# Keys on 128 partitions, all seven slots of P turned by DMA, q in 1 KB packets turned by TensorE, and the expert stage spread over later pairs

## The chip, the cores and the metric

One core of one Trainium2 chip runs the whole program. Its compute engines are TensorE (PE in the profile; PEld is its weight load), VectorE (DVE), ScalarE (ACT) and GpSimd (POOL). SyncE (SP) computes nothing here: it issues every DMA, one after the other, and waits on semaphores in that same order. The metric is the device time of one execution in microseconds, the median of several runs. A profiled execution gives the trace.

## The reference, cut to what matters

Attention for 8 batches of 12 heads, 448 positions and head size 64, with an RMS norm on q and k; then, on the heads of a batch joined to 768 columns, an expert block: a product with `w_in` (768 x 1024), a relu, a convolution of three taps along the sequence, a gate, and a product with `w_out` (1024 x 768). All in float32.

```python
q_n, k_n = (rmsnorm(q, g_q), rmsnorm(k, g_k))
scores = scale * np.matmul(q_n, k_n.transpose(0, 1, 3, 2))
scores = scores - np.max(scores, axis=-1, keepdims=True)
attn = np.exp(scores)
attn = attn / (np.sum(attn, axis=-1, keepdims=True) + 1e-09)
attn_out = np.matmul(attn, v)
...
h = np.maximum(x @ w_in, 0.0)
for k in range(K):
    conv_out += conv_w[k][None, None, :] * hp[:, k:k + S, :]
gate = 1.0 / (1.0 + np.exp(-conv_out))
return (h * gate @ w_out).astype(np.float32)
```

## The kernel before, in words

**Pairs.** Two heads are one pair: 48 pairs, 6 to a batch. Both heads of a pair lie beside each other (2 x 64 rows of the array), and the 2 x 448 = 896 query positions of a pair are cut into seven slots of 128. In a float16 product each operand is split into a high and a low half (`hi`, `lo`), and three of the four half products are summed: about 22 bits for three float16 passes.

**One pair.** `load_k` and `load_q` fetch k and q (224 KB each) to 112 partitions, four key positions to a partition (`PB = 112`, `NB = 4`). `square`, `square_sum` and `rsqrt` make the norm's factor, `apply_rms` multiplies with it. Then k goes through PE: `qk_transpose` makes four transposes into one bank, `qk_hi` (ACT or DVE) and `qk_lo` (DVE) take the halves out. For q this holds up to pair 6; from pair 7 on (`nq=7`) q is split first on the input side (`x_cast`, `x_rest`) and turned by a DMA transpose (`x_turn`, 8 blocks of 112 x 128). q is loaded with "(h t p)", so in packets of 256 bytes. `scores` makes the products, `soft_max` the row's maximum (DVE), `soft_exp` the exponentials and their sums (ACT).

**P.** For the product with v the exponentials of a slot (128 queries x 448 keys) have to be turned. Up to pair 9 all seven slots go through PE: `p_transpose` (four float32 transposes), `p_evac` (a copy from the bank to `PT`), and `pv` multiplies in float32, four key blocks of 112. From pair 10 on (`n1=10`) five of the seven slots (`dg=5`) go another way: `p_hi` rounds to float16, `p_lo` takes the rest, both into a buffer `ph` (three of them) padded to 4 + 4 blocks of 128 columns, and `p_turn` turns the buffer by one DMA transpose into `PT`. `pv` then multiplies in float16: three half products x four key blocks x two heads = 24 matmuls of 320 columns. The other two slots still use `p_transpose` and float32 products (8 matmuls of 128 columns).

**The end of a pair.** The sums are inverted, turned by PE (`sum_transpose`), copied to `rT` (`sum_evac`), stored to DRAM (`sum_store`, tile `rd`) and read back spread over 64 rows (`sum_load`, tile `rB`); `x_scale` multiplies the product with them, `x_hi` and `x_lo` split the result for the expert block.

**Expert block.** For each batch, `in_part` (8 chunks of 18 matmuls of 448 columns), the elementwise chain `in_relu` to `in_lo` on DVE, ACT and POOL, then `out_part` (matmuls of 384 columns) and `out_evac`, `out_store`.

**What sets the order.** The program is written step by step by a planner. Each step has a due time (`at(...)`, from `base(n)`, the start of pair n, and numbers in `PH`), the steps that it must follow (`needs`), engines it may run on with a cost (`options`), and latencies (`LAT`). The planner simulates the engines and takes the step that can start first; `BETA` times the due time is added, so that of two ready steps the one due earlier goes first. The result is one fixed order for each engine and for SP; nothing is chosen at run time. `plan_moe` sets the due times of the expert block: it begins `ti` after the end of the batch's last pair, a chunk of `in_part` lasts `si`, a unit of `out_part` lasts `so`, the same in every batch.

## Time and profile before

| | us |
|---|---|
| median of 3 runs | 883.89 (881.51 to 886.46) |
| profiled execution, whole | 889.08 |
| its span on the core | 887.0 |
| start of the first exponential of pair 10 | 188.07 |
| start of the first exponential of pair 47 | 796.58 |

The profile of one execution has three stages. Up to 188 us the weights are loaded and split, and pairs 0 to 9 run with all slots through PE. From 188 to 797 us pairs 10 to 47 run, with the expert block of the earlier batches between them. Behind that stands the expert block of the last batch, nearly alone. Busy time of an engine is the union of its instructions; matmuls are pipelined, so the time of one matmul in the chain of work that ended last is shorter than its own duration. SP's instructions are not counted as busy, but the trace has when it issued each DMA, how long that took, and what it waited for.

### The profile page before, as it was taken

What the parts mean: (1) busy time and instruction counts of PE and PEld (TensorE: products, weight loads), DVE (VectorE), ACT (ScalarE), POOL (GpSimd) and SP (SyncE); (2) the same over time, 40 slices, a digit from 0 to 9 for tenths busy, and PEclk for the clock granted to TensorE, in tenths of its full rate; (3) what the DMA queues carried; (4) which work ended last, traced back from release to release, by engine and by line L of the source; (5) the groups of instructions that cost most, each with busy time, mean ns of one, the idle gap of its engine ahead of it and who ended that gap; (6) DMA issues with size and microseconds to landing.
All of it is one profiled execution on the core that took longest, in us unless ns stands there. A gap on an engine that the chain in (4) does not pass through costs nothing.

```text
span 887.0 us, 18246 instructions
## 1 busy us (share of the span) xinstructions
PE 827.4 (93%) x6260; PEld 478.1 (54%) x6260; DVE 702.6 (79%) x1267; ACT 666.8 (75%) x1543; POOL 591.8 (67%) x721
## 2 busy tenths in 40 slices
...
PEclk9897999999999999999999999999999999999999
DMA  8944442257896798798896998577896896565001
GB/s 256 266 124 140 138 83 66 70 111 150 184 201 133 146 197 182 127 163 149 195 182 129 155 208 161 124 171 152 188 180 128 170 187 143 111 109 113 18 18 54
DMA packets 324072, 128.25 MB, mean 145 GB/s; under 512 B 287012, under 2 KB 322188, under 8 KB 323212
## 3 DMA queue, kind: packets, MB, share of 16 engines
...
## 4 chain that ended last, share of the span: by engine, by line
PE 59%; DVE 10%; POOL 8%; DMA 8%; ACT 7%; issue 5%; SPq 1%; ACTq 0%; POOLq 0%; DVEq 0%
PE bank L895 18%; PE bank L816 16%; PE bank L608 9%; PE bank L651 5%; PE bank L744 5%; PE bank L735 5%; DMA PT<-ph 4%; DMA rB<-rd 2%; PE bank L464 2%; POOL sq L90 2%; DMA qT<-qkf 1%; POOL ph L90 1%; ACT ph L78 1%; POOL wo L296 1%; ACT sq L354 1%
## 5 line engine op out<-in xcount | busy, mean ns | idle before, releaser
L816 PE MATMUL bank<-x,wi 128*128 128x448 f16 x1152 | 241.4, 353 | 0.0
L895 PE MATMUL bank<-wo,gring 128*128 128x384 f16 (+1 forms) x1056 | 204.5, 327 | 0.8 <-DVE kT L482 0.8
L816 PEld LDWEIGHTS <-wi 128*128 128x128 f16 x1152 | 109.8, 98 | 99.7 <-issue 13.0
L895 PEld LDWEIGHTS <-gring 128*128 128x128 f16 (+1 forms) x1056 | 101.2, 99 | 65.5 <-issue 10.4
L608 PE MATMUL bank<-kT,qT 64*128 64x448 f16 x864 | 105.1, 359 | 5.6 <-DVE qT L484 3.9
L90 POOL TENSOR_TENSOR sq<-qkf,st 112x512 f32<-112x512 f32 x88 | 99.5, 1148 | 8.9 <-DVE st L389 7.2
L78 ACT COPY PT<-bank 112x512 f32<-112x512 f32 x138 | 79.8, 584 | 23.4 <-PE bank L651 22.8
L735 PE MATMUL bank<-PT,v 112*64 112x128 f32 (+1 forms) x768 | 78.4, 342 | 1.1 <-ACT PT L78 0.8
L90 POOL TENSOR_TENSOR x<-rB,x 128x448 f16<-128x448 f32 x48 | 51.1, 1064 | 27.4 <-ACT x L78 25.9
L744 PE MATMUL bank<-PT,vp 112*64 112x320 f16 x912 | 68.4, 299 | 0.0
L608 PEld LDWEIGHTS <-qT 64*128 64x128 f16 x864 | 34.5, 95 | 55.8 <-issue 27.5
L367 DVE TENSOR_REDUCE st<-sq 112x16 f32<-112x1024 f32 x48 | 57.7, 1209 | 6.9 <-ACT sq L354 6.7
L493 POOL COPY qz<-qT 64x128 f16<-64x128 f16 x91 | 34.1, 375 | 38.1 <-DMA qT<-qkf 11.3
L735 PEld LDWEIGHTS bank<-PT,v 112*64 112x64 f32 x768 | 43.1, 138 | 28.5 <-issue 17.5
L744 PEld LDWEIGHTS <-vp 112*64 112x64 f16 x912 | 53.0, 110 | 7.3 <-DMA PT<-ph 0.2
L751 DVE TENSOR_TENSOR rB<-bank,rB 128x448 f32<-128x448 f32 x48 | 29.7, 619 | 26.8 <-DMA rB<-rd 13.7
L464 PE MATMUL bank<-ident,sq 112*128 112x112 f32 x220 | 33.2, 276 | 18.2 <-POOL sq L90 17.3
L895 PE MATMUL bank<-wo,wi 128*128 128x384 f16 (+1 forms) x192 | 46.9, 326 | 0.0
L354 ACT ACTIVATE sq<-qkf 112x1024 f32<-112x1024 f32 x36 | 38.1, 1059 | 9.3 <-DMA qkf<-in_q_dram 8.2
L90 POOL TENSOR_TENSOR qkf<-sq,qkf 112x512 f16<-112x512 f32 x30 | 35.2, 1175 | 13.1 <-ACT qkf L78 13.0
L714 DVE SCALAR_TENSOR_TENSOR vp<-v,vsc,vp 112x512 f16<-112x512 f32 x38 | 41.6, 1094 | 0.6 <-ACT vp L82 0.6
L464 PEld LDWEIGHTS bank<-ident,sq 112*128 112x128 f32 x220 | 25.7, 148 | 28.4 <-POOL sq L90 20.2
...
## 6 DMA issues: line engine op xcount, KB each, us to landing
...
PT<-ph SPq DMA_TRANSPOSE x190
rd<-rT SPq DMA_DIRECT2D x48, 3.5 KB
```

Source lines behind the costliest of these rows:

```text
L78: (nc.scalar.copy if e == "ACT" else elementwise(e).tensor_copy)(dst, src)
L90: elementwise(e).tensor_tensor(dst, a, b, op=op)
L354: nc.scalar.activation(sq, old("qkf", n), AF.Square)
L367: nc.vector.tensor_reduce(old("st", m)[:, 0, n - m].rearrange("p i s -> p (i s)"), old("sq", n).rearrange("p i h t d -> p (i h t) d")[..., ...
L464: nc.tensor.transpose(ps[:, t * PB : (t + 1) * PB], x[:, t], ident[:PB, :PB])
L608: nc.tensor.matmul(ps[u][:, :S], lhs, kt[r, w], start=(i == 0), stop=(i == 2))
L651: nc.tensor.transpose(ps[:PB, kt * P : (kt + 1) * P], e[:, kt * PB : (kt + 1) * PB], ident)
L714: nc.vector.scalar_tensor_tensor(vp[:, 1], old("v", n), old("vsc", n // NP)[:PB, 1:2], vp[:, 0], op0=ALU.mult, op1=ALU.subtract,)
L735: nc.tensor.matmul(ps[HALF[h], out[h]], v[:, h, k], pt[:, k, col[h]], start=(k == 0), stop=(k == NB - 1),)
L744: nc.tensor.matmul(ps[HALF[h], out[h]], v[:, w, h, k], pt[:PB, a, k, col[h]], start=(i == 0 and k == 0), stop=(i == 2 and k == NB - 1),)
L816: nc.tensor.matmul(ps[:, :S], wi[:, wl, c, fc * P : (fc + 1) * P], old("x", b * NP + c)[:, xl], start=(i == 0), stop=(i == 3 * NP - 1),)
L895: nc.tensor.matmul(ps[p0 : p0 + m, :NO2], g, wo[:, wl, fc, half * NO2 : (half + 1) * NO2], start=(i == 0), stop=(i == 3 * NFC - 1),)
```

## The change

Five things are changed, and with them numbers of the planner.

1. **Keys on 128 partitions.** k and v of a head are no longer four positions on 112 partitions each. The first 256 positions lie on partitions 0 to 63 (four each), the other 192 on partitions 64 to 127 (three each). A load of k becomes two DMAs; a load of v becomes three, since the fourth place of the upper partitions is filled with a copy. A key block is now 128 keys (three and a half blocks), so `qk_transpose` of k makes three transposes of 128 and one of 64, `p_transpose` works on 128 keys at a time, and float32 `pv` takes only the upper half of the last block. Buffers of k and q are fixed (`qkbuf`), and the places that no load fills are zeroed once at the start.
2. **All seven slots by DMA** from pair 10 on (`dg=7`): no `p_transpose`, no `p_evac` and no float32 product there. The buffer holds 3.5 + 3.5 blocks, so `p_turn` moves 7 blocks of 128 and not 8; `p_lo` becomes two instructions of 384 and 64 columns. `pv` becomes 11 matmuls a head, 22 a pair, of 448 columns. There are four `ph` buffers, not three.
3. **q through PE in all pairs** (`nq=100`): `x_cast`, `x_rest` and `x_turn` are gone, `qk_transpose`, `qk_hi` and `qk_lo` of q take their place. q is then loaded with "(h p t)", in packets of 1 KB.
4. **The expert stage spread**: `si` and `so` are multiplied by numbers of each batch (`si0` to `si7`, `so0` to `so7`, up to 1.79), and `so` grows from 6.862 to 8.54.
5. **Small**: three `rB` buffers, not two; `g_rows`, `cw_in` and `cw_rows` lie in the end of `gring`; costs in `options`, some `LAT` entries and `PH` numbers.

```diff
-    ... nf=2, ... dg=5, n1=10, ... nq=7, nk=97, ... so=6.862
+    ... nf=3, ... dg=7, n1=10, ... nq=100, nk=97, ... so=8.54
+    si0=1.0, si1=1.6, si2=1.625, si3=1.415, si4=1.633, si5=1.364, si6=1.149, si7=1.079,
+    so0=1.0, so1=1.536, so2=1.613, so3=1.631, so4=1.791, so5=1.264, so6=1.071, so7=1.0,
...
-        rB=2, ... ph=3, vp=2,
+        rB=3, ... ph=4, vp=2,
...
-    phbuf = [const.tile([P, 2, 4, P], F16, name=f"ph{i}") for i in range(BUFS["ph"])]
+    phbuf = [const.tile([P, 2 * S], F16, name=f"ph{i}") for i in range(BUFS["ph"])]
+    qkbuf = [const.tile([P, 2, 2, 4, D], F32, name=f"qk{i}") for i in range(BUFS["qkf"])]
...
     def load_k(n):
-        queue("lk").dma_start(x[:, 1], kf[rows].rearrange("(h p t) d -> p h t d", h=2, t=NB))
+        for i, m in enumerate((4, 3)):
+            queue("lk").dma_start(
+                x[HALF[i], 1, :, :m],
+                src[:, 256 * i : 256 * i + 64 * m].rearrange("h (p t) d -> p h t d", t=m),
+            )
...
     def load_q(n):
-            old("qkf", n)[:, 0], qf[rows].rearrange("(h t p) d -> p h t d", h=2, t=NB)
+        order = "(h t p) d -> p h t d" if turned(n, 0) else "(h p t) d -> p h t d"
+            old("qkf", n)[:PB, 0], qf[rows].rearrange(order, h=2, t=NB),
...
     def v_load(n):
-        queue("lv").dma_start(t, vf[rows].rearrange("(h p t) d -> p h t d", h=2, t=NB))
+        for i, m in enumerate((4, 3)):
+            queue("lv").dma_start(
+                t[HALF[i], :, :m],
+                src[:, 256 * i : 256 * i + 64 * m].rearrange("h (p t) d -> p h t d", t=m),
+            )
+        queue("lv").dma_start(
+            t[HALF[1], :, 3], src[:, :256].rearrange("h (p t) d -> p h t d", t=4)[:, :, 3]
+        )
...
     def p_lo(n, j):
-        binary(
-            on["p_lo", n, j], ph[:, 1, :, :PB],
-            old("e", (n, j)).rearrange("q (k p) -> q k p", k=NB), ph[:, 0, :, :PB], ALU.subtract,
-        )
+        for k0, k1, to in ((0, 3 * P, 4 * P), (3 * P, S, S)):
+            binary(
+                on["p_lo", n, j], ph[:, to : to + k1 - k0], e[:, k0:k1], ph[:, k0:k1],
+                ALU.subtract,
+            )
...
-    PV3 = ((0, 0), (0, 1), (1, 0))
+    PV7 = (
+        ((0, 0, P), (1, 0, P), (2, 0, P), (3, 0, P)),
+        ((0, 1, P), (1, 1, P), (2, 1, P), (3, 1, 64)),
+        ((4, 0, P), (5, 0, P), (6, 0, P)),
+    )
...
     def plan_moe(b):
-        si, so = PH["si"], PH["so"]
+        si, so = PH["si"] * PH[f"si{b}"], PH["so"] * PH[f"so{b}"]
...
+        for z in qkbuf:
+            nc.gpsimd.memset(z[96:, 0], 0.0)
+            nc.gpsimd.memset(z[HALF[1], 1, :, 3], 0.0)
```

What this does to the fixed order is seen best around one pair. SP first: the rows between the store of the sums of pair 26 (`rd_26`) and that of pair 27, before. `PT_27` are the turned slots of pair 27, `qT_28` and `qT_29` turned q of later pairs, `v_34` and `qkf_31` loads ahead.

```order
L686 DMA rd_26_6231<-rT_26_6218 7x128
L692 DMA rB_26_6267<-rd_26_6231 64x448 x2
L455 DMA_TRANSPOSE qT_28_6289<-qkf_28_5689 128x8x112
L643 DMA_TRANSPOSE PT_27_6306<-ph1_72 128x8x128
L643 DMA_TRANSPOSE PT_27_6306<-ph2_73 128x8x128
L643 DMA_TRANSPOSE PT_27_6306<-ph0_71 128x8x128
L526 DMA v_34_6384<-in_v_dram 112x2x256
L343 DMA qkf_31_6389<-in_k_dram 112x2x256
L347 DMA qkf_31_6389<-in_q_dram 112x8x64
...
L686 DMA rd_27_6506<-rT_27_6489 7x128
```

The same place of the change, its first rows; `qk1` and `qk2` are the fixed buffers of k and q.

```order
L714 DMA rd_26_6168<-rT_26_6158 7x128
L352 DMA qk1_75<-in_k_dram 64x2x256
L352 DMA qk1_75<-in_k_dram 64x2x192
L673 DMA_TRANSPOSE PT_27_6202<-ph3_73 128x7x128
L720 DMA rB_26_6216<-rd_26_6168 64x448 x2
L673 DMA_TRANSPOSE PT_27_6202<-ph0_70 128x7x128
L360 DMA qk1_75<-in_q_dram 112x2x256
...
L546 DMA v_34_6302<-in_v_dram 64x2x256
L546 DMA v_34_6302<-in_v_dram 64x2x192
L550 DMA v_34_6302<-in_v_dram 64x2x64
...
L714 DMA rd_27_6426<-rT_27_6390 7x128
```

Between the stores of the sums of pairs 10 and 47, SP has 221 transposes and 251 other DMAs before, 259 and 344 after; a pair goes from 6.0 and 6.8 to 7.0 and 9.3.

PE, what stands there for the turning and multiplying of pair 27 and the turning of pair 28's q and k (`sq_28`), before; `rsum_27` are the sums, `bank2_6501` the product.

```order
L464 MATMUL bank7_6262<-ident_69,sq_28_5904 128x112 x4
...
L651 MATMUL bank0_6426<-ident_69,e_(27_5_6407 112x128 x4
...
L651 MATMUL bank4_6454<-ident_69,e_(27_6_6434 112x128 x4
...
L673 MATMUL bank2_6467<-ident_69,rsum_27_6252 7x128
...
L735 MATMUL bank2_6501<-PT_27_6306,v_27_4730 64x128 x8
...
L744 MATMUL bank2_6501<-PT_27_6306,vp_27_6220 64x320
```

After; the last row stands 22 times, the last one before 24 times.

```order
L479 MATMUL bank3_6170<-ident_68,sq_28_5921 128x128 x3
L479 MATMUL bank3_6170<-ident_68,sq_28_5921 128x64
...
L479 MATMUL bank6_6188<-ident_68,sq_28_5921 128x112 x4
...
L701 MATMUL bank1_6377<-ident_68,rsum_27_6144 7x128
...
L786 MATMUL bank1_6524<-PT_27_6202,vp_27_6128 64x448
```

The two turned slots (L651) and the float32 product (L735) are gone, four transposes of q (`128x112 x4`) are new. The expert matmuls stand elsewhere: between the sum transposes of pairs 10 and 19, of 19 and 28, of 28 and 37 and of 37 and 47 there were 332, 232, 300 and 316 matmuls of `out_part`, and there are now 216, 264, 300 and 392; those of `in_part` stay within 3.

POOL, the rests of pair 27's slots, before and then after.

```order
L90 TENSOR_TENSOR ph1_72<-e_(27_0_6253,ph1_72 128x4x112
L90 TENSOR_TENSOR gring_81<-c_(3_3_6189,gring_81 128x448
L90 TENSOR_TENSOR ph2_73<-e_(27_1_6281,ph2_73 128x4x112
L90 TENSOR_TENSOR ph0_71<-e_(27_2_6303,ph0_71 128x4x112
L493 COPY qz0_74<-qT_28_6289 64x2x64 x2
```

```order
L94 TENSOR_TENSOR ph3_73<-e_(27_0_6145,ph3_73 128x384
L94 TENSOR_TENSOR ph3_73<-e_(27_0_6145,ph3_73 128x64
L94 TENSOR_TENSOR ph0_70<-e_(27_1_6166,ph0_70 128x384
L94 TENSOR_TENSOR ph0_70<-e_(27_1_6166,ph0_70 128x64
L94 TENSOR_TENSOR sq_29_5962<-qk2_76,st_28_5955 128x2x4x64
```

Over the whole program POOL has 231 rests in two pieces each after, where it had 180 in one, and DVE has 35 where it had 10.

More of the change, by code (lines that the diff above doesn't have):

```diff
@@ L463, in qk_transpose @@
         for t in range(NB):
-            nc.tensor.transpose(ps[:, t * PB : (t + 1) * PB], x[:, t], ident[:PB, :PB])
+            m = min(P, S - t * P) if i else PB
+            nc.tensor.transpose(
+                ps[:, t * P : t * P + m] if i else ps[:, :S].rearrange("c (p t) -> c t p", t=NB)[:, t],
+                x[:m, t], ident[:m, :m],
+            )
     def qk_tiles(n, i):
@@ L719, in heads @@
     def heads(n, k0):
-        wt = (NS - nd(n)) * P // 2
-        if k0 < NB:
-            return (slice(0, wt), slice(S - wt, S)), (slice(0, wt), slice(wt, 2 * wt))
-        wd = S - wt
-        return (slice(wt, S), slice(0, wd)), (slice(0, wd), slice(wd, 2 * wd))
+        part = sorted(SLOTS[nd(n) :] if k0 < NB else SLOTS[: nd(n)])
+        cols = [c * P for c in part]
+        sides = []
+        for h in range(2):
+            mine = [
+                (max(c, h * S) - h * S, min(c + P, (h + 1) * S) - h * S, i * P + max(h * S - c, 0))
+                for i, c in enumerate(cols) if c + P > h * S and c < (h + 1) * S
+            ]
+            if mine:
+                w = sum(b - a for a, b, _ in mine)
+                assert mine[-1][1] - mine[0][0] == w
+                sides.append((
+                    h, slice(mine[0][0], mine[-1][1]), slice(mine[0][2], mine[0][2] + w)
+                ))
+        return sides
     def pv(n, k0):
@@ L729, in pv @@
             new_bank("m", ("v", n))
-        ps, (out, col) = bank("m", ("v", n)), heads(n, k0)
+        ps, sides = bank("m", ("v", n)), heads(n, k0)
         if k0 < NB:
@@ L733, in pv @@
             for k in range(k0, k0 + PV_STEP):
-                for h in range(2):
+                r = slice(64 * (k == NB - 1), P)
+                for h, out, col in sides:
                     nc.tensor.matmul(
-                        ps[HALF[h], out[h]], v[:, h, k], pt[:, k, col[h]],
+                        ps[HALF[h], out], v[r, h, k], pt[r, k, col],
                         start=(k == 0), stop=(k == NB - 1),
@@ L739, in pv @@
             return
-        i = k0 - NB
-        (a, w), v, pt = PV3[i], old("vp", n), places(n)[1]
-        for k in range(NB):
-            for h in range(2):
+        i, v, pt = k0 - NB, old("vp", n), places(n)[1]
+        for c, w, m in PV7[i]:
+            for h, out, col in sides:
                 nc.tensor.matmul(
-                    ps[HALF[h], out[h]], v[:, w, h, k], pt[:PB, a, k, col[h]],
-                    start=(i == 0 and k == 0), stop=(i == 2 and k == NB - 1),
+                    ps[HALF[h], out], v[:m, w, h, c % 4], pt[:m, c, col],
+                    start=(i == 0 and c == 0), stop=(i == 2 and c == 6),
                 )
@@ L1315, in options @@
             keep_cw=lambda: [dve(0.2), act(0.25)],
-            load_k=lambda: [dma("lk", 0.75)],
-            load_q=lambda: [dma("lq", 1.1)],
+            load_k=lambda: [dma("lk", 0.41, 2)],
+            load_q=lambda: [dma("lq", 1.36 if turned(a[0], 0) else 0.8)],
             square=lambda: [act(1.06), pool(1.9)],
```

127 lines of the change are left out of this document (72 added, 55 removed).

## The prediction

> **What bounds the kernel now.** First the page: busy time by engine, the granted clock and the DMA share in 40 slices, and the engines of the chain of work that ended last.
>
> ```profile
> PE 827.4 (93%) x6260; PEld 478.1 (54%) x6260; DVE 702.6 (79%) x1267; ACT 666.8 (75%) x1543; POOL 591.8 (67%) x721
> PEclk9897999999999999999999999999999999999999
> DMA  8944442257896798798896998577896896565001
> PE 59%; DVE 10%; POOL 8%; DMA 8%; ACT 7%; issue 5%; SPq 1%; ACTq 0%; POOLq 0%; DVEq 0%
> ```
>
> PE leads, but 93% is a mean. So I cut the trace where pairs 10, 19, 28, 37 and 47 begin (timeline of ACT: the first exponential of each) and ask for busy time by stretch.
>
> ```profile
> 188.07 0.64 ACT L620 ACTIVATE e_(10_0_2156<-bank,sst_(10_0_2138 128x448 f32<-128x448 f32 x1
> 332.25 0.63 ACT L620 ACTIVATE e_(19_0_4311<-bank,sst_(19_0_4301 128x448 f32<-128x448 f32 x1
> 483.61 0.63 ACT L620 ACTIVATE e_(28_0_6509<-bank,sst_(28_0_6491 128x448 f32<-128x448 f32 x1
> 632.85 0.63 ACT L620 ACTIVATE e_(37_0_8714<-bank,sst_(37_0_8705 128x448 f32<-128x448 f32 x1 [2.81 <-DVE sst_(37_0_8705 L612]
> 796.58 0.63 ACT L620 ACTIVATE e_(47_0_11131<-bank,sst_(47_0_11122 128x448 f32<-128x448 f32 x1 [0.68 <-DVE sst_(47_0_11122 L612]
> 188.00:332.00 144.00, 140.84 (x1143) 82.60 (x1142) 126.16 (x234) 114.36 (x271) 111.32 (x139) 1.00 0.85 167
> 332.00:484.00 152.00, 149.17 (x1169) 88.59 (x1169) 129.33 (x233) 124.05 (x290) 113.44 (x137) 1.00 0.86 163
> 484.00:633.00 149.00, 145.43 (x1189) 86.64 (x1186) 124.30 (x225) 116.41 (x277) 109.82 (x136) 1.00 0.82 165
> 633.00:797.00 164.00, 161.95 (x1307) 94.83 (x1305) 133.56 (x248) 137.15 (x322) 119.53 (x144) 1.00 0.75 147
> sum 609.00, PE 597.39 PEld 352.65 DVE 513.36 ACT 491.96 POOL 454.11; mean PE 149.35 PEld 88.16 DVE 128.34 ACT 122.99 POOL 113.53
> ```
>
> After the length stand PE, PEld, DVE, ACT and POOL, then clock, DMA share and GB/s. PE is busy 98% of these 608.5 us at full clock: 37 pairs at 16.45 us, set by PE. Per pair DVE has 13.9, ACT 13.3, POOL 12.3 us of work and the DMA engines 0.82 x 16.45 = 13.5.
>
> SP is not on that list. It issues in order, so I read its own timeline where it stands closest, and its issue times by line (minimum/median/maximum in ns).
>
> ```profile
> 308.17 4.04 SPq L643 DMA_TRANSPOSE PT<-ph  x3
> 312.26 0.66 SPq L909 DMA_DIRECT2D out_dram<-c_('o'_1_0_1_3937  x1
> 313.01 0.38 SPq L526 DMA_DIRECT2D v<-in_v_dram  x1
> 313.49 0.44 SPq L343 DMA_DIRECT2D qkf<-in_k_dram  x1
> 313.98 0.45 SPq L347 DMA_DIRECT2D qkf<-in_q_dram  x1
> 314.50 2.16 SPq L643 DMA_TRANSPOSE PT<-ph  x1
> ...
> 325.35 0.50 SPq L526 DMA_DIRECT2D v<-in_v_dram  x1
> L643 SPq DMA_TRANSPOSE PT<-ph x190: 1231/1274/2622, 192.9 to 807.9; - x190
> L455 SPq DMA_TRANSPOSE qT<-qkf x41: 1221/1234/1955, 120.2 to 781.3; - x41
> ```
>
> Three turns in a row take (312.26 - 308.17)/3 = 1.36 us each; the small DMAs behind them follow every 0.48 to 0.75, 0.53 in the mean of a pair. At these unstalled prices a pair of before (6.0 turns, 6.8 others) asks 11.7 us of SP. From 305.70 to 325.35, 9 turns and 10 others take 19.65 us; unstalled they would take 17.5. So the burst price is 1.12 times that: the turn behind v, k and q takes 2.16.
>
> **The change, by parts.** *PE, per pair from 10 on.* Pieces of the chain: start, length, what.
>
> ```profile
> 271.02 0.39 PE bank L464 x4
> 275.95 1.02 PE bank L735 x16
> 276.98 1.63 PE bank L744 x24
> 279.28 2.94 PE bank L816 x15
> 282.22 0.44 PE bank L651 x4
> 290.58 1.42 PE bank L895 x16
> 311.57 0.65 PE bank L895 x4
> ```
>
> Gone: two turned slots, 2 x 0.44, and the float32 product, 1.02 (its 8 matmuls leave 16 records). The float16 product goes from 24 x 320 to 22 x 448 columns: 1.63 x 22/24 x 448/320 = 2.09, +0.46. q through PE: +0.39. k's transposes still stream 448 columns. Sum -1.05; 37 pairs give -38.9. An expert matmul costs 2.94/15 = 0.196 (`in_part`), 0.65/4 = 0.163 (`out_part`, 128 positions) or 1.42/16 = 0.089 (64 positions).
>
> *The expert stage.* It only moves in PE's order. With the counts of the order, PE needs in the four stretches, keeping its idle time of before: 144.2 - 9.5 - 116 x 0.163 + 0.6 = 116.4; 151.4 - 9.5 + 112 x 0.163 - 80 x 0.089 - 0.6 = 152.4; 149.2 - 9.5 - 80 x (0.163 - 0.089) - 0.6 = 133.2; 163.7 - 10.5 + 76 x 0.163 + 0.6 = 166.2. The gain stands in stretches one and three, where attention is to run ahead of the experts, and only if everything else can do 9 pairs there in 116 and 133 us.
>
> *SP.* In the four stretches stand 63 turns and 89 others, 63 and 92, 63 and 91, 70 and 72 (55 and 68, 53 and 60, 54 and 67, 59 and 56 before). That 7 blocks are issued faster than 8 isn't seen: 112 rows a block cost 1234, 128 rows 1274. Unstalled: 132.9, 134.4, 133.9, 133.4; at the burst price 148.8, 150.6, 150.0, 149.5. So **SP takes over from PE in stretches one and three**. Which price? The stalls follow loads: q's 896 packets become 224, a turn has one block less, but there are more DMAs. Nearest is the median row, so I take a quarter of the stall, 1.03: 136.9 and 137.9. Bounds: a turn priced by blocks, 7/8 of 1.36 (below), and 1.12.
>
> *Other engines*, rows by line and shape, POOL's piece from the chain:
>
> ```profile
> L90 POOL TENSOR_TENSOR qkf<-sq,qkf 112x512 f16<-112x512 f32 x30 | 35.2, 1175 | 13.1 <-ACT qkf L78 13.0
> L484 DVE TENSOR_TENSOR qT<-bank,qT 128x448 f16<-128x448 f32 x7 | 4.3, 611 | 0.0
> L392 POOL TENSOR_TENSOR st<-st 112x32 f32<-112x32 f32 x24 | 6.3, 263 | 2.0
> 244.69 1.05 POOL ph L90
> ```
>
> POOL: a rest in two pieces isn't in this trace; between 1.05 (no fixed cost) and 1.05 + 0.26 (a whole small instruction more), I take 1.2. 231 x 1.2 - 180 x 1.05 - 30 x 1.175 = +53, 1.4 a pair: 13.7. DVE: 41 rests of q (+25), 25 more rests of P (about +28), 11 of q's fewer (-11) and some shifts: about 14.7. ACT trades 72 copies of `PT` for 72 casts and stays. All are hidden by 15.2 us of SP a pair; at 14.7 DVE's cover is thin, and a late maximum would cost what it is late. DMA: 49 blocks a pair for 47, fewer q packets, two thirds of a load more: 13.5 stays.
>
> *Start and end.* The first loads wait for zeroed buffers, six fills on POOL: 0 to 2 us late; q's larger packets may give the same back: 0, bounds -2 and +2. Pairs 7 to 9 lose the turn of q that stood on the chain:
>
> ```profile
> 179.10 5.42 DMA qT<-qkf
> SPq L686 <- ACT rT L82: 36.5, 16, 5.2
> 80.00:120.00 40.00, 34.33 (x202) 16.93 (x199) 36.40 (x52) 31.30 (x74) 26.00 (x29) 0.87 0.46 137
> ```
>
> (The other two rows are used below.) Between 0 and -5.4, I take -3. Behind pair 47's sums stand 16 more matmuls of `out_part`, +2; the landing of its last turn lies beside the 84 matmuls left of batch 6.
>
> *Sum.* 136.9 + 152.4 + 137.9 + 166.2 = 593.4 for 608.5: -15.1; with -3 + 2, -16.1. From the profiled execution's own 889.1: 873.0. That execution stood 5.2 above the median of the runs shown, so **868**.
>
> **The rivals.** *A: PE keeps the pace.* A turn might be issued block by block: 7/8 of 1.36 is 1.19, SP has 122.1 and 123 us in stretches one and three, and there 122.1 and 133.2 count: 573.9, -35.6 in all, **848**. The Trainium skill ("DMA: Bandwidth & Descriptors", "Why a DMA increments its semaphore by 16 and not by 1") lists for earlier generations 262,144 cycles of sequencer time for a transpose of 8,192 tiles within SBUF, a price by the tile; by it this rival holds. Against it speaks the pair 1234 and 1274: 12.5% fewer rows, 3% less time.
>
> *B: nothing is left.* At a price of 1.10 SP needs 146.2 and 147.3: 612.1 in all, **887**, no change. From 1.09 on the gain is gone. For it: SP has 37% more of the small DMAs, and nothing shows that they stall less.
>
> *C, slower: SP queues behind the store of the sums.* The store waits for `rT`, and all turns of the next pair stand behind it. In the stretch from pair 10 to 47 SP waited 36.5 us there (second row above), about 1 us a pair; today that is hidden in SP's slack. In a stretch that SP sets it isn't: at the burst price 148.8 + 9 and 150 + 9, 635.4 in all, **910**. It decides as soon as such a stretch takes longer than before, over 16.4 us a pair. Against it: an SP that is late finds `rT` ready.
>
> *D: the clock falls.* Where PE had work for 34.33 of 40 us the granted clock was 0.87 (third row). Stretch three at 0.87 takes 133.2/0.87 = 153, 15 more than my sum: **883**. Stretch one, 134, would still be SP's. The Trainium skill ("TensorE: Matmul & The Clock Gate", "Why this matters for your kernels") wants no gaps of PE over some 3 us; by that rule D needs its waits in one piece, and the 5.7 us of this row could be.
>
> **How the numbers follow.** A measurement of this kernel tells about 0.5% (4.4 us) from no change. Forecast (857 to 879) 0.46, A 0.17, B 0.13, C 0.20, D 0.04: faster 0.63, same 0.17, slower 0.20. The range 847 to 896 leaves out the end of A (0.08) and the upper half of C (0.11).
>
> **What would show it.** Right: in the profile after, issue rows of 266 turns with a median near 1.25; SP nearly without gaps between pairs 10 and 19 and 28 and 37, at about 15.2 us a pair; PE below 90% there, 97% in the other two stretches. A: a median near 1.1 and PE at 97% throughout. C: long waits of SP for `rT` or `ph`, and a POOL or ACT that waits for turns. D: a granted clock below 0.95 after 188 us. Wrong altogether: if stretch two or four, where PE has as much work as before, changes by more than 5 us, or if DVE, not SP, is what PE waits for.

## The result, and the profile after

| | before | after |
|---|---|---|
| median | 884.79 us (881.51 to 886.46, 4 runs) | 917.37 us (914.52, 916.34, 918.40 and 2093.56) |
| ratio | 1 | 1.036, interval 1.0315 to 1.041 |
| profiled execution, its span | 889.08, 887.0 | 916.34, 914.5 |

One run took 2093.56 us; it is in that median and not in the ratio, and without it the median is 916.34. The change makes the kernel 3.6% slower; the prediction, 868 with a range of 847 to 896, is 49 us too low. The same lines of the page as before: busy time, granted clock and DMA share in 40 slices, and the engines of the chain that ended last.

```profile
PE 829.8 (91%) x5436; PEld 424.1 (46%) x5436; DVE 738.2 (81%) x1330; ACT 674.2 (74%) x1571; POOL 643.3 (70%) x984
PEclk9999899999999799999999999999999999999999
DMA  8773422136887787887788688887788888566001
PE 44%; DVE 18%; POOL 11%; DMA 9%; issue 6%; ACT 6%; SPq 4%; POOLq 0%; DVEq 0%; ACTq 0%
```

PE is as busy as before (829.8 for 827.4 us), but its share of the chain fell from 59% to 44%. Cut at the same pairs, by the first exponentials on ACT's timeline:

```profile
194.42 0.64 ACT L652 ACTIVATE e_(10_0_2213<-bank,sst_(10_0_2199 128x448 f32<-128x448 f32 x1
342.77 0.63 ACT L652 ACTIVATE e_(19_0_4223<-bank,sst_(19_0_4174 128x448 f32<-128x448 f32 x1
499.37 0.64 ACT L652 ACTIVATE e_(28_0_6412<-bank,sst_(28_0_6401 128x448 f32<-128x448 f32 x1
646.42 0.61 ACT L652 ACTIVATE e_(37_0_8547<-bank,sst_(37_0_8521 128x448 f32<-128x448 f32 x1
821.12 0.61 ACT L652 ACTIVATE e_(47_0_11028<-bank,sst_(47_0_11004 128x448 f32<-128x448 f32 x1
```

and the busy time by stretch (PE, PEld, DVE, ACT, POOL, then clock, DMA share, GB/s):

```profile
194.00:343.00 149.00, 132.84 (x878) 62.72 (x877) 123.89 (x238) 116.79 (x276) 115.13 (x188) 0.94 0.76 156
343.00:499.00 156.00, 148.12 (x961) 74.49 (x961) 143.75 (x244) 123.36 (x292) 126.79 (x202) 0.99 0.79 166
499.00:646.00 147.00, 139.00 (x968) 71.30 (x968) 128.31 (x239) 116.33 (x284) 125.69 (x195) 1.00 0.80 165
646.00:821.00 175.00, 171.25 (x1167) 87.69 (x1162) 147.29 (x269) 141.96 (x335) 140.38 (x218) 0.99 0.78 151
```

PE fills 98% of the fourth stretch (99% before), but only 89, 95 and 95% of the first three. What stands there instead is SP. Its timeline near pair 17, start and length of each issue:

```profile
305.97 2.58 SPq L673 DMA_TRANSPOSE PT<-ph  x2
308.65 0.54 SPq L360 DMA_DIRECT2D qk<-in_q_dram  x1
309.30 2.56 SPq L673 DMA_TRANSPOSE PT<-ph  x2
311.96 0.43 SPq L714 DMA_DIRECT2D rd<-rT  x1
313.83 0.50 SPq L720 DMA_DIRECT2D rB<-rd  x1
315.92 1.24 SPq L673 DMA_TRANSPOSE PT<-ph  x1
317.20 0.58 SPq L720 DMA_DIRECT2D rB<-rd  x1
317.89 4.57 SPq L673 DMA_TRANSPOSE PT<-ph  x3
322.51 1.33 SPq L352 DMA_DIRECT2D qk<-in_k_dram  x2
323.88 1.26 SPq L546 DMA_DIRECT2D v<-in_v_dram  x2
325.18 0.60 SPq L550 DMA_DIRECT2D v<-in_v_dram  x1
```

Two waits of 1.4 and 1.6 us stand behind 312 and 314 us; else each issue follows the one ahead by about 0.1 us. Added up in this way over a whole stretch, SP issues for 128.9, 138.7 and 131.5 us of the first three (148.4, 156.6 and 147.0 long); with the steps of up to 0.2 us between issues it is 140.0, 151.3 and 143.2, and only 7.0, 4.7 and 4.4 us are longer waits. Before, these waits were 25.6, 33.7 and 32.4 us. Where the time goes, against the forecast (us; the last column is the first experiment below):

| stretch | before | forecast | after | off | K and V by one DMA each |
|---|---|---|---|---|---|
| up to pair 10 | 188.1 | 185.1 | 194.4 | +9.3 | 190.8 |
| pairs 10 to 18 | 144.2 | 136.9 | 148.4 | +11.5 | 136.6 |
| 19 to 27 | 151.4 | 152.4 | 156.6 | +4.2 | 151.1 |
| 28 to 36 | 149.2 | 137.9 | 147.0 | +9.1 | 138.2 |
| 37 to 46 | 163.7 | 166.2 | 174.7 | +8.5 | 173.0 |
| behind | 90.4 | 92.4 | 93.4 | +1.0 | 93.7 |

### The profile page after: what moved, and what is told of

Its sections match the earlier page's. It is cut to its first block, busy times and chain, and to the rows that moved or that the text cites. A ratio compares the mean times of both kernels' runs of the same rounds, so it can differ in the third digit from the quotient of the medians.

```text
span 914.5 us, 17424 instructions
## 1 busy us (share of the span) xinstructions
PE 829.8 (91%) x5436; PEld 424.1 (46%) x5436; DVE 738.2 (81%) x1330; ACT 674.2 (74%) x1571; POOL 643.3 (70%) x984
## 4 chain that ended last, share of the span: by engine, by line
PE 44%; DVE 18%; POOL 11%; DMA 9%; issue 6%; ACT 6%; SPq 4%; POOLq 0%; DVEq 0%; ACTq 0%
PE bank L858 14%; PE bank L937 13%; PE bank L640 5%; PE bank L786 4%; POOL ph L94 4%; DMA rB<-rd 4%; PE bank L479 3%; DMA PT<-ph 3%; POOL sq L94 2%; DVE ph L94 2%; PE bank L778 2%; DMA qk<-in_q_dram 2%; PE bank L681 2%; SPq L673 2%; ACT ph L82 1%
## 5 line engine op out<-in xcount | busy, mean ns | idle before, releaser
L786 PE MATMUL bank<-PT,vp 128*64 128x448 f16 (+1 forms) x836 | 102.0, 368 | 8.6 <-DMA PT<-ph 8.1
L94 POOL TENSOR_TENSOR sq<-qk,st 128x512 f32<-128x512 f32 (+1 forms) x87 | 95.6, 1115 | 3.4 <-PE bank L640 0.7
L479 PE MATMUL bank<-ident,sq 112*128 112x112 f32 (+2 forms) x384 | 63.9, 280 | 23.3 <-POOL sq L94 17.9
L786 PEld LDWEIGHTS <-vp 128*64 128x64 f16 (+1 forms) x836 | 44.1, 110 | 61.2 <-issue 38.6
L380 DVE TENSOR_REDUCE st<-sq 128x16 f32<-128x1024 f32 x48 | 58.0, 1210 | 17.1 <-ACT sq L367 14.8
L479 PEld LDWEIGHTS bank<-ident,sq 112*128 112x128 f32 (+2 forms) x384 | 47.3, 145 | 48.4 <-POOL sq L94 19.5
L82 ACT COPY PT<-bank 128x512 f32<-128x512 f32 x66 | 38.3, 584 | 11.9 <-PE bank L681 11.9
L367 ACT ACTIVATE sq<-qk 128x1024 f32<-128x1024 f32 x32 | 33.8, 1057 | 13.7 <-DMA qk<-in_q_dram 12.5
L937 PE MATMUL bank<-wo,carry 128*64 128x384 f16 x192 | 36.6, 333 | 1.6 <-ACT rT L86 1.1
L778 PE MATMUL bank<-PT,v 128*64 128x448 f32 (+1 forms) x160 | 36.5, 563 | 1.6 <-DVE kT L500 1.1
```

The source lines that it names most:

```text
L82: (nc.scalar.copy if e == "ACT" else elementwise(e).tensor_copy)(dst, src)
L94: elementwise(e).tensor_tensor(dst, a, b, op=op)
L367: nc.scalar.activation(sq, old("qkf", n), AF.Square)
L380: nc.vector.tensor_reduce(old("st", m)[:, 0, n - m].rearrange("p i s -> p (i s)"), old("sq", n).rearrange("p i h t d -> p (i h t) d")[..., ...
L479: nc.tensor.transpose(ps[:, t * P : t * P + m] if i else ps[:, :S].rearrange("c (p t) -> c t p", t=NB)[:, t], x[:m, t], ident[:m, :m],)
L778: nc.tensor.matmul(ps[HALF[h], out], v[r, h, k], pt[r, k, col], start=(k == 0), stop=(k == NB - 1),)
```

## The experiments

Theory **SP**: the time of SP's own issues paces pairs 10 to 36. Rivals: the rest of P in two pieces on POOL and VectorE; the loop of turn, landing and release of a `ph` buffer; the spread of the expert stage; bytes and packets instead of issues. Theory **tile shape** (of a matmul, the rows and columns of the array that it uses), for the rest: TensorE saved less than forecast since its matmuls change shape in mid-chain. Lengths are cut by the first exponentials, as above; of the ratios (to the kernel before, on the same chip) the interval is given. The kernels called f try to win the time back. Runs whose edit touches nothing ahead of pair 10 (e2, e3, e9) have it at 191.3 to 193.8 and the changed kernel at 194.4, so 3 us there tell little.

| kernel | median us | ratio | pair 10 at | 10-18 | 19-27 | 28-36 | 37-46 |
|---|---|---|---|---|---|---|---|
| after | 917.4 | 1.0315 to 1.0410 | 194.4 | 148.4 | 156.6 | 147.0 | 174.7 |
| e1 one DMA | 886.9 | 0.9996 to 1.0046 | 190.8 | 136.6 | 151.1 | 138.2 | 173.0 |
| e2 rest whole | 909.0 | 1.0227 to 1.0301 | 193.8 | 145.7 | 154.2 | 145.5 | 174.1 |
| e3 PV shape | 914.6 | 1.0292 to 1.0381 | 191.3 | 148.8 | 156.8 | 148.6 | 172.4 |
| e4 no spread | 920.4 | 1.0359 to 1.0448 | 192.6 | 146.8 | 161.4 | 154.1 | 173.5 |
| e5 V on ACT | 942.7 | 1.0638 to 1.0684 | 215.5 | 145.9 | 157.8 | 151.9 | 175.9 |
| e6 turns 128 | 908.3 | 1.0228 to 1.0301 | 192.6 | 149.1 | 156.1 | 145.9 | 173.4 |
| e7 three | 925.2 | 1.0441 to 1.0481 | 211.7 | 147.0 | 151.9 | 145.9 | 173.9 |
| e8 before, cut | 903.2 | 1.0171 to 1.0223 | 189.8 | 146.0 | 157.5 | 154.0 | 163.4 |
| e9 fifth buffer | 917.5 | 1.0333 to 1.0399 | 192.3 | 148.4 | 157.1 | 149.6 | 175.2 |
| e10 V for two | 903.9 | 1.0156 to 1.0246 | 191.5 | 143.9 | 153.4 | 146.0 | 176.6 |
| f4 light | 892.6 | 1.0054 to 1.0119 | 194.5 | 142.2 | 146.8 | 143.0 | 169.9 |
| e11 first ten | 908.8 | 1.0225 to 1.0292 | 186.0 | 149.4 | 156.5 | 147.3 | 174.5 |
| e12 tiny DMAs | 943.8 | 1.0619 to 1.0684 | 199.6 | 153.5 | 162.8 | 154.3 | 177.6 |
| f6 eight blocks | 889.9 | 1.0031 to 1.0068 | 184.4 | 142.5 | 152.4 | 142.3 | 172.6 |
| f7 and V for two | 879.9 | 0.9907 to 0.9957 | 188.7 | 140.2 | 146.0 | 139.7 | 169.9 |
| f8 first ten singly | 878.2 | 0.9877 to 0.9927 | 184.8 | 141.1 | 146.7 | 137.8 | 171.0 |
| e13 before, q by PE | 900.2 | 1.0112 to 1.0166 | 192.2 | 145.6 | 153.5 | 150.5 | 164.6 |
| e14 before, cut at 64 | 913.6 (one run) | | 188.6 | 151.2 | 162.4 | 155.1 | 163.9 |

**e1: fewer DMAs.**

```diff
-        for i, m in enumerate((4, 3)):
-            queue("lk").dma_start(x[HALF[i], 1, :, :m], ...)
+        queue("lk").dma_start(
+            x[:, 1], bass.AP(src.tensor, src.offset, [[3 * D, P], [S * D, 2], [D, 4], [1, D]])
+        )
```

V in the same way, for its three. This kernel leaves out the last keys of each head. It also has fewer packets of V, which e10 and e12 set apart from the issues.

> The changed kernel, but K of a pair comes by one DMA instead of two and V by one instead of three (128 partitions, 4 rows each, the rows of neighbouring partitions overlap, so the last keys of a head are never read and others are read twice); order of every engine as it was. Theory SP (its queue of DMA issues paces the stretches of pairs 10 to 36): three plain DMAs at 0.67 us from start to start go from every pair, 2.0 us a pair, more than the gap to TensorE's need, so TensorE becomes the bound there: the three stretches 148.4, 156.6 and 147.0 fall towards TensorE's busy time of 132.8, 148.1 and 139.0, to about 138, 152 and 143, and the run goes from 917 to 890 to 903. Rival POOL/DVE (the rest of P in two pieces on POOL and VectorE paces them): 912 to 917.

The busy times of the first three stretches, in the same columns:

```profile
190.80:327.40 136.60, 126.32 (x869) 61.34 (x869) 122.79 (x234) 116.00 (x276) 115.41 (x186) 0.98 0.84 171
327.40:478.40 151.00, 146.14 (x972) 74.97 (x968) 140.91 (x247) 123.72 (x293) 128.88 (x206) 1.00 0.87 178
478.40:616.60 138.20, 135.65 (x960) 69.08 (x959) 127.93 (x239) 116.09 (x284) 123.62 (x192) 1.00 0.89 175
```

The chain of its page, where PE is back at more than before:

```profile
PE 63%; DVE 17%; POOL 7%; ACT 5%; DMA 4%; issue 4%; SPq 1%; POOLq 0%; ACTq 0%; DVEq 0%
```

The stretches go where the theory put them, and a little further (886.9, under its range of 890 to 903), with POOL's and VectorE's work as in the changed kernel: 30.5 of the 33 us are gone. PE takes 92, 97 and 98% of them, and SP's waits are back to 15.9, 22.0 and 15.4 us. The fourth stretch stays at 173.0: that one was PE's.

**e2: the rest of P in one instruction.** `p_lo` is `binary(on["p_lo", n, j], ph[:, S:], e, ph[:, :S], ALU.subtract)`.

> The changed kernel with the rest of P formed by one instruction of 448 columns, in straight order (its blocks then do not lie where PV looks for them); order of every engine as it was. It takes 0.2 to 0.3 us from each of the 266 slots on POOL or VectorE, about 1.7 us a pair. Theory SP: the waits of the turn on POOL (76.6 us in all) shrink, but the queue stays full in the stretches of pairs 10 to 36: 908 to 917. Rival POOL/DVE: these stretches fall by 1 to 1.7 us a pair, 27 to 45 us in all: 872 to 890.

Busy time by engine, from its page:

```profile
PE 828.0 (91%) x5436; PEld 424.0 (47%) x5436; DVE 717.3 (79%) x1295; ACT 673.6 (74%) x1571; POOL 607.1 (67%) x753
```

57 us of work are gone (21 on DVE, 36 on POOL). The three stretches lose 6.6 us in all, the kernel about 8. That is the theory's range; the two pieces are a second, small cost.

**e3: one shape in the PV chain.** `(3, 1, 64)` becomes `(3, 1, P)`.

> The changed kernel with the one PV matmul pair of 64 rows (low V by high P, block 3) widened to 128 rows, as its neighbours are (it adds the product of the two low parts). No other edit. Theory tile shape (two switches of the PV chain's tile shape cost about 0.1 us each, from 187 ns a row to 286 and 304 ns): PV falls from 2.45 to about 2.2 us a pair; seen in the stretch of pairs 37 to 46, which TensorE paces, as -2 us, and with pairs 47 and the other stretches mostly hidden behind SP: 912 to 916. Rival (the odd steps are waits for data and not the shape): 917.

The chain pieces of one pair, of the changed kernel and then of this one:

```profile
710.49 2.44 PE bank L786 x22
```

```profile
709.04 2.20 PE bank L786 x22
```

The 0.24 us is as expected, and so is the fourth stretch at -2.3; the other stretches did not fall. The widened pair costs nothing, the two switches did: in the median of the last twelve pairs the chain steps from one pair of matmuls to the next in 186 ns, into the pair of 64 rows in 282 and out of it in 303, and in 186 and 185 at the same places here.

**e4: no spread.** All `si*`, `so*` are 1, all `ti*`, `to*` 0, `so=6.862`.

> The changed kernel with the expert stages not spread: all factors on their steps 1, their offsets 0, and the step of the second stage 6.862 as before; the order is planned anew. Theory SP: the stretches' sum stays what SP's issues need, since these are the same in number; a stage packed tighter gives TensorE 163 instead of 152 us in some pairs and less in others: 910 to 930. Rival spread (the spread is what costs the time): 885 to 900.

The four stretches sum to 635.9 for 626.7, the end is 4 us shorter. The spread is not what costs; without it the kernel is about as slow.

**e5: V's DMAs on ScalarE.** `queue("lv")` in `v_load` becomes `nc.scalar`.

> The changed kernel with the three DMAs of V issued by ScalarE instead of SP, each at its place in the order; same DMAs, same packets, same data. Theory SP (it is the time of SP's own issues that paces pairs 10 to 36): the three stretches fall as with the merged DMAs, from 148.4, 156.6 and 147.0 to about 138, 152 and 140, less what ScalarE loses by three issues a pair (it is busy 74 % of the span): 885 to 900. Rival packets (K and V in more and smaller packets slow the transfers, and the merged DMAs only had fewer of them): 912 to 920.

Outside both ranges. SP's waits in the three stretches grow to 22.8, 25.3 and 28.7 us, yet these do not fall (455.6 us in all, for 452.0), and the time up to pair 10 grows by 21 us. Taken alone, that speaks against theory SP. ACT feeds every slot (`soft_exp`, most of `p_hi`), and three issues of 0.61 us a pair now stand in its own queue. This run tells nothing on issues against packets, since it loads another engine of the same chain; that ACT paces there is argued, not shown.

**e6: the transposes of K and Q on 128 rows.** `ps[...]` from `x[:, t]` with the whole `ident`, `apply_rms` of Q on all 128 rows.

> The changed kernel with all eight transposes of a pair's K and Q on 128 rows (Q's had 112, K's last 64; the rows added hold zeros), so that the tile shape does not change among them. Theory tile shape: K and Q fall from 1.11 to about 0.85 us a pair; seen in the stretch of pairs 37 to 46 as -2 to -3 us and little in the others, 912 to 916. Rival (the transposes wait for VectorE or POOL, not for the shape): 917.

Chain pieces of K's and Q's four in the changed kernel, then here:

```profile
702.98 0.53 PE bank L479 x4
704.18 0.38 PE bank L479 x4
```

```profile
718.16 0.44 PE bank L479 x4
719.24 0.44 PE bank L479 x4
```

0.91 becomes 0.88: the theory was right for K (0.53 to 0.44), but Q goes from 0.38 to 0.44 with its larger blocks. That is not the 0.25 expected. The fourth stretch fell by 1.3. The median is 9 us lower, more than any stretch of the profiled execution (912.32) shows, so that much is not explained.

**e7: e3, e5 and e6 together.**

> The changed kernel with three edits together: V's DMAs issued by ScalarE, the PV chain all on 128 rows, the transposes of K and Q all on 128 rows. If SP paced pairs 10 to 36 and TensorE is what comes next, TensorE's savings now show in every pair, 0.2 + 0.25 us on some 44 pairs, about 20 us below the kernel with V alone moved: 866 to 882. If something else comes next (ScalarE, POOL): no faster than the kernel with V alone moved.

17.5 us below e5, near the 20 expected of TensorE's savings (12.7 of the profiled execution's gain lie in the four stretches), but far over the range, since that was built on e5.

**e8: the kernel before, with K and V cut.**

```diff
+        for r in (slice(0, 40), slice(40, 80), slice(80, PB)):
+            queue("lv").dma_start(t[r], src[r])
...
+        for r in (slice(0, PB // 2), slice(PB // 2, PB)):
+            queue("lk").dma_start(x[r, 1], src[r])
```

> The kernel before, with K's one DMA cut in two and V's one cut in three by partitions (same bytes, same packets of 1 KB, same data). Theory SP: the issues cost SP 3 x 0.6 us a pair, 16 to 18 us a stretch of nine pairs, and SP's waits there were 26 to 43 us, so the room is still there: 884 to 892. Rival split (that the parts are issued apart costs the time, whatever SP's room): about 3 us a stretch and more at the start, 895 to 910.

The rival's range, and a correction of the theory: SP still waits 18.3, 28.9 and 26.4 us in the three stretches, and they are 1.8, 6.1 and 4.8 us longer. An SP with waits left is not free. The turns stand in its queue in order, so whatever is issued ahead of one delays it. In the trace, ACT waits 41.7 us between pairs 10 and 36 for a turn to land and free its `ph` buffer (31.4 in the kernel before), and PE's idle time there, mostly waits for ACT's exponentials, goes from 9.6 to 18.0 us; that this is the whole path is argued, not shown.

**e9: a fifth `ph` buffer.**

> The changed kernel with five buffers instead of four for the halves of P that wait for their turn; order of every engine as it was. Theory SP (the number of issues on its queue paces pairs 10 to 36): POOL and ScalarE run further ahead and wait less for a buffer, but the queue needs the same time: 910 to 917. Rival loop (the turn, its landing and the release of its buffer make a loop that paces POOL and SP together): one buffer more breaks it, 885 to 900.

917.5, half a microsecond over the theory's range and far from the rival's: the loop is refuted.

**e10: V for two pairs at once.**

```diff
+        t = vbuf[n // 2 % len(vbuf)]
+        if n % 2 == 0:
+            return
+        rows = slice((n - 1) * 2 * S, (n + 1) * 2 * S)
+        src = vf[rows].rearrange("(h k) d -> h k d", h=4)
```

> The changed kernel with V loaded for two pairs at once: three DMAs for two pairs instead of six, same bytes and packets, and its largest value taken of two pairs by one instruction; the rest as it was. Theory SP: 1.5 plain DMAs go from a pair, 1.0 us of its queue, 9 us a stretch down to what TensorE needs (about 137, 152 and 143): the stretches of pairs 10 to 36 lose 16 to 20 us in all, the start 1 to 3: 895 to 903. Rival packets (the packets that the parts make pace, not the issues): 912 to 917.

903.9, just over the theory's range. -8.7 us in the three stretches, about half of what was expected, with bytes and packets unchanged. SP's waits there grow to 11.7, 11.0 and 11.3 us, so a part of the freed time turned into waits.

**f4: lighter on SP and PE** (e10, e3, e6, and `nc.vector.tensor_copy(x[HALF[1], :, 3], x[HALF[0], :, 3])` for V's third DMA).

> The changed kernel with V loaded for two pairs at once and its doubled rows copied by VectorE instead of a third DMA, the PV chain all on 128 rows, and the transposes of K and Q all on 128 rows. Two issues go from each pair, 1.3 us of SP's queue, and 0.2 + 0.1 us of TensorE. If SP's issues pace pairs 10 to 36 and TensorE is what comes next: 872 to 886, faster than both kernels or level with the one before. If the size of packets or the loop of buffers paces: above 900.

892.6 is between the two ranges. The second stretch is 9.8 us shorter than in the changed kernel, but pair 10 starts no earlier.

**e11: the first ten pairs in the old layout.** `if n < PH["n1"]`: K and V by one DMA each to 112 partitions, four transposes of 112, `p_transpose` of 112.

> The changed kernel with K and V of the first ten pairs laid on 112 partitions by one DMA each, as before the change (their P goes through TensorE and needs no other layout); pairs 10 to 47 as changed. Theory SP issues at the start: three issues fewer on each of the first pairs bring pair 10 back from 194.4 to 188 to 190 us, the rest stays: 911 to 914. Rival (the first ten pairs lose by the zeroing of buffers on POOL, or are thrown back by what follows them): 916 to 918.

Pair 10 comes at 186.0, 8.4 us sooner, and the median falls by 8.6, both further than expected. The stretches behind stay. So the first ten pairs lose by the new layout of K and V; the zeroing of buffers, still there on POOL, isn't it. That the issues are the cause does not follow. e1, with whole loads in the new layout, has pair 10 at 190.8, so they are worth about 3.6 us, and in the changed kernel SP has 105 us of waits there. The layout also changes TensorE's blocks: up to pair 10 PE is busy for 150.1 us in the changed kernel, 147.5 in e1 and 144.8 here. How the rest divides is open.

**e12: three tiny DMAs more.** Behind V's: `queue("lv").dma_start(tiny3[:, (3 * n + i) % 48], vf[rows][i : i + 1, :8])`, `i` from 0 to 2.

> The changed kernel with three more plain DMAs a pair on SP, each of one packet of 32 bytes, behind V's. Theory SP issues: each costs the queue its issue and step, about 0.6 us, whatever it moves: 1.8 us a pair, +16 us in each of the stretches of pairs 10 to 36, less in that of pairs 37 to 46, where SP waits 26 us: 965 to 985. Rival bytes and packets (the transfers pace, not the issues): 917 to 922.

Issue times (minimum/median/maximum, ns), V's third piece and the tiny ones:

```profile
L551 SPq DMA_DIRECT2D v<-in_v_dram x48: 595/605/1207, 24.3 to 741.3; - x48
L555 SPq DMA_DIRECT2D tiny<-in_v_dram x144: 223/250/452, 26.7 to 742.7; - x144
```

Neither range. Bytes are refuted: 32 bytes a DMA cost the kernel 26 us. But an issue has no one price: a tiny one takes 0.25 us, a piece of V 0.61. SP's issues and steps grew by 6.3, 11.4 and 7.7 us in the three stretches, these by 5.1, 6.2 and 7.3. What paces is SP's time, not the number of its issues.

**f6: eight blocks.** From pair 10 on `ph` holds 448 + 64 zeros + 448 + 64 zeros, so `p_lo` is one instruction and V's doubled rows aren't needed; PV takes 12 blocks on 128 rows. With e6 and e11.

```diff
+        binary(on["p_lo", n, j], ph[:, 4 * P : 4 * P + S], e, ph[:, :S], ALU.subtract)
...
+        for c, w in (((c, 0) for c in range(4)), ((c, 1) for c in range(4)), ((c, 0) for c in range(4, 8)))[i]:
```

> Pairs 0 to 9 as in the kernel with 112 partitions there; from pair 10 on P's halves in eight blocks with zeros behind each half, so that the rest of P is one instruction and V needs no doubled rows (two DMAs a pair, 12 pairs of PV matmuls on 128 rows instead of 11); transposes of K and Q on 128 rows. One issue less a pair for SP, 1.7 us less a pair on POOL and VectorE, about nothing on TensorE: 888 to 900 if both theories hold in part; 905 and more if neither the halves' rest nor one issue counts.

889.9, 27 us below the changed kernel: 10.0 up to pair 10, 16.8 in the four stretches. It has one issue less a pair and 1.7 us less on POOL and VectorE.

**f7: f6 with V for two pairs**, each bound taken two pairs later.

> The kernel with eight blocks, and V loaded for two pairs at once, its largest value taken two pairs later: two issues a pair fewer than in the changed kernel. If SP's issues pace first and POOL and VectorE next, TensorE paces nearly everywhere: 872 to 886. If something else paces: not below the kernel with eight blocks alone.

879.9, below the kernel before, with 14.0 us less in the four stretches than f6; pair 10 is 4.3 us later than there.

**f8: f7, the first ten pairs' V loaded singly.**

> The kernel with eight blocks and V for two pairs at once, but the first ten pairs load their V pair by pair, and its largest value is taken pair by pair. If the start of that kernel (pair 10 at 188.7 us, 184.4 in the kernel with eight blocks alone) is V's later arrival, 4 us come back: 874 to 878. If not: 879 to 881.

878.2, at the upper end of what was expected, with pair 10 back at 184.8: the start was V's later arrival; of the 4 us, 1.8 show in the median. It beats both kernels, 0.7 to 1.2% below the one before. Its DMA share in 40 slices, from the page:

```profile
DMA  8963522248999999999998899999999998666001
```

The DMA engines now are close to full as well. K's issues in two shapes, 112 partitions (pairs 0 to 9) and 64:

```profile
L353 SPq DMA_DIRECT2D qk<-in_k_dram x10: 312/359/1546, 2.8 to 106.9; - x10
L356 SPq DMA_DIRECT2D qk<-in_k_dram x76: 595/621/1076, 109.5 to 722.5; - x76
```

**e13: one part alone**, in the kernel before: `nq=100`, Q in 1 KB packets.

> The kernel before with one part of the change alone: Q of all pairs in 1 KB packets and through TensorE (its turn goes from SP's queue, its cast and rest from ScalarE, POOL and VectorE, its two evacuations come); planned anew. Theory TensorE (the kernel before is paced by TensorE in pairs 10 to 47, and four transposes cost it 0.5 us a pair): +0.5 us on 41 pairs, 897 to 910. Rival room (a turn less on SP and less on POOL give back as much): 880 to 890.

Busy time and chain, from its page:

```profile
PE 843.2 (94%) x6424; PEld 494.0 (55%) x6424; DVE 703.0 (78%) x1294; ACT 667.3 (74%) x1554; POOL 576.5 (64%) x697
PE 74%; DVE 13%; ACT 4%; DMA 3%; POOL 2%; issue 2%; SPq 1%; ACTq 0%; DVEq 0%; POOLq 0%
```

PE does 15.8 us more and the kernel takes 12.9 us more (than the one before on the same chip), although SP now waits 45 to 54 us in each of the first three stretches. The number came as expected, its parts only in part: of the profiled execution's 11.6 us, 4.1 come up to pair 10, 1.8 at the end and 5.7 in the four stretches, 0.15 a pair where 0.5 was priced. In each of the first three stretches PE is busy 3 to 4 us longer and idle 1.4 to 2.3 us less. So where TensorE paces it pays for Q, and gets a part back.

**e14: the price of a shape.** The kernel before, K cut at partition 64, V at 32 and 64, one line each.

> The kernel before, with K cut at partition 64 (64 and 48 partitions) and V at 32 and 64 (32, 32 and 48); it is for the issue rows alone. In the changed kernel a piece of 64 partitions never took less than 0.595 us, with 128 or with 256 packets; K cut into 56 and 56 in the kernel before took 0.315 at least and 0.397 in the median. Theory shape (64 partitions are what makes the piece dear): here the first piece of K takes 0.595 at least, the others 0.25 to 0.35 at least. Rival load (the pieces are dear because SP's queue in the changed kernel is full): all pieces 0.28 to 0.35 at least, 0.33 to 0.42 in the median.

K's 64 and 48, then V's 32, 32 and 48:

```profile
L344 SPq DMA_DIRECT2D qkf<-in_k_dram x48: 601/651/1782, 2.2 to 761.1; - x48
L345 SPq DMA_DIRECT2D qkf<-in_k_dram x48: 579/592/665, 2.9 to 761.9; - x48
L529 SPq DMA_DIRECT2D v<-in_v_dram x48: 311/430/1414, 23.9 to 713.2; - x48
L530 SPq DMA_DIRECT2D v<-in_v_dram x48: 312/419/1567, 24.4 to 713.8; - x48
L531 SPq DMA_DIRECT2D v<-in_v_dram x48: 412/418/453, 24.8 to 714.3; - x48
```

The load of the queue is refuted: in a kernel whose SP waits 21 to 31 us a stretch, the 64-partition piece takes 0.601 at least. For the others, expected at 0.25 to 0.35 at least, it fails: the 48 of K behind it take 0.579, the 48 of V 0.412. Cut at 64, K costs SP 0.65 + 0.59 = 1.24 us; cut at 56 in e8, twice 0.397, with the same bytes and packets. What makes the piece dear, its 64 partitions or something that comes with them, stays open; the second piece, of 48, is nearly as dear.

## Why the prediction was wrong

Of the 43.3 us between 873.0 and 916.34 (the rest of the 49.4 are the 5 us taken off and 1.0 to the median), the table of stretches has 20.6 in the two stretches that SP was to pace, 12.7 in the two of PE, 9.3 up to pair 10 and 1.0 behind; 0.3 less stood outside the span.

**SP takes over: right in kind, mis-sized.** The failed term is the price of SP's queue: "Unstalled: 132.9 ... I take a quarter of the stall, 1.03". The turn was right: 266 turns, 1220/1243/2280 ns, for the 1.25 foretold. The others were not. The issues that were new took:

```profile
L352 SPq DMA_DIRECT2D qk<-in_k_dram x96: 595/606/1431, 2.2 to 761.7; - x96
L546 SPq DMA_DIRECT2D v<-in_v_dram x96: 595/626/1550, 22.7 to 713.8; - x96
L550 SPq DMA_DIRECT2D v<-in_v_dram x48: 597/605/1131, 24.0 to 714.5; - x48
```

From start to start a plain DMA takes 0.66 us in the mean of the first stretch (0.58 and 0.08), where I took 0.53. With the counts that the stretch really held, 61 turns and 83 others, my price gives (83.0 + 44.0) x 1.03 = 130.8; the 0.114 more on each of 83 others is 9.5, and the 7.0 of waits, which I had at zero, makes 147.3, for 148.4. The price was taken over all shapes of before. Its rows held a warning: K and V on 112 partitions, and `rB` on 64:

```profile
L343 SPq DMA_DIRECT2D qkf<-in_k_dram x48: 312/422/2330, 2.2 to 736.4; - x48
L526 SPq DMA_DIRECT2D v<-in_v_dram x48: 317/520/2492, 22.9 to 688.1; - x48
L692 SPq DMA_DIRECT2D rB<-rd x96: 444/578/1499, 55.8 to 814.0; - x96
```

The new pieces have 64 partitions. At the row nearest in shape, 0.58 and not 0.42 to 0.52, five new issues a pair cost 2.9 where two cost 0.94. Shape is not all of it. Q, on 112 partitions in the changed kernel too, took

```profile
L360 SPq DMA_DIRECT2D qk<-in_q_dram x48: 319/578/667, 3.6 to 765.8; - x48
```

where it had 0.45 before. In pairs 10 to 46 of the kernel before, V and Q took 0.53 and 0.57 in the median right behind a turn, but 0.38 and 0.45 where another plain issue stood ahead; in the changed kernel Q takes 0.58 and 0.59 at such places. So what stands ahead of an issue counts too.

Put as one factor on 1.36 a turn and 0.53 a plain DMA, by the counts that the stretches held, SP's issues and steps came to 1.10 in each of the first three, to 1.04 to 1.06 in e1 and to 1.08 to 1.09 in the kernel before. So 1.03 was nearly right for the change without its pieces, and the pieces made it 1.10.

That e1's stretches, 136.6, 151.1 and 138.2, meet the forecast of 136.9, 152.4 and 137.9 is luck in the first and the third. The forecast has SP set them; in e1 SP waits 15.9 and 15.4 us there, and PE is busy for 126.3 and 135.7 us, where the prediction gave it 116.4 and 133.2 with its idle time. So PE's need in stretch one is a second term that came out too small. One reason shows: matmuls were counted between sum transposes, the time was cut at first exponentials. Cut like the time, the stretch holds 252 matmuls of `out_part` for 334 before, 82 fewer and not 116, or 5.5 us at 0.163.

**TensorE saves 1.05 a pair: wrong, about 0.57.** "1.63 x 22/24 x 448/320 = 2.09" became 2.44, since one pair of 64 rows stands in the middle of the chain; e3 gives 0.24 of the 0.35 back. "k's transposes still stream 448 columns" and "q through PE: +0.39" make 0.78; the pieces take 0.53 + 0.38 = 0.91. Together 0.48 a pair, 4.8 us on the ten pairs of the fourth stretch, which is 8.5 over; e1 leaves 6.8 of these. In the trace the stretch also holds 82 more matmuls of `out_part` than before and not 76 (1.0 us at 0.163), and PE's idle time went from 2.0 to 3.7 us; about 1 us stays open.

**Stretch two.** 4.2 over; SP's 151.3 us of issues came up to PE's 152.4. That neither had room would explain it, and is not shown.

**Up to pair 10: the sign was wrong.** "Pairs 7 to 9 lose the turn of q", -3, and "0" for the start. e11 shows 8.4 us that the new layout of K and V costs there, of which e1 leaves about 3.6 to the issues. The prediction priced that layout from pair 10 on and put it at nothing in the first ten. The -3 is not confirmed: without the layout pair 10 stands at 186.0, 2.1 before the 188.1, but in e13, with Q by PE alone, at 192.2, 4.1 behind it.

**POOL and VectorE.** 13.7 and 14.7 us a pair were forecast; the rows above make (115.1 + 126.8 + 125.7 + 140.4)/37 = 13.7 and 543.2/37 = 14.7. "All are hidden" is wrong by the 8 us of e2. Of the signs, the median of the turns and an SP nearly without gaps came; its 15.2 us a pair were 16.5 and 16.3 in stretches one and three, and PE was at 95% in stretches two and three, for the 97% and the less than 90% foretold.

**The rivals.** A is refuted: seven blocks of 128 took 1243 ns for 1274 of eight. The rule for earlier generations that stood beside it (the Trainium skill, "DMA: Bandwidth & Descriptors", "Why a DMA increments its semaphore by 16 and not by 1") gives a price by the tile; this trace shows 31 ns for the eighth block, where A needs 170. B's price, 1.10, is the one that came, and its 146.2 and 147.3 us stand beside 148.4 and 147.0, in part by luck: in stretch one its counts are 6.6 us too high and its waits 7.0 too low. Its 887 is too low by the other stretches and the start, and that e1 is at 886.9 is chance. C gave the side, at 910, but not the cause: in the first stretch a store of sums waits once, 4.3 us, and the other waits are short ones of turns for POOL (SP's waits there: us in total, times, longest):

```profile
SPq L673 <- POOL ph L94: 14.3, 17, 1.3
...
SPq L714 <- ACT rT L86: 4.3, 1, 4.3
```

Its point of decision, 16.4 us a pair, was reached in stretch one (148.4/9 = 16.5), through the price of issues, and just missed in stretch three (16.3). D: its sign came in stretch one, a clock of 0.94, but its price stood on stretch three, where the clock was 1.00. At full clock PE's 132.84 us in stretch one would be 124.9, an estimate, so the clock has 8.0 us there at most; e1 gained 11.8 us there with the clock at 0.98, so the two were not separated. "Wrong altogether: if stretch two or four changes by more than 5 us" came true: +5.2 and +11.0.
